# First dense pair in chunks of 512, 512 and 128 tokens, with a fourth accumulator and PSUM banks handed out by first free

## The chip, the cores and the metric

The kernel runs on one core of a Trainium2 chip. The metric is the device time of one execution in microseconds (us). The engines are PE (TensorE), DVE (VectorE), ACT (ScalarE), POOL (GpSimd) and SP (SyncE, which issues DMAs). PSUM, into which PE writes, has eight banks, each of which holds 512 float32 columns on 128 partitions.

## What is computed

An attention step makes 4608 tokens of 512 numbers; each token is routed to one of 8 experts, exactly 576 to each, in the order of the largest gate values that are left; the expert's two layers act on its tokens; then one dense network with a hidden width of 2048 acts on all of them.

```python
def _moe_ref(x, w_gate, w1, w2):        # x 4608 x 512, 8 experts, cap 576
    ...
    out[mask] = np.maximum(x[mask] @ w1[e], 0.0) @ w2[e]

def _moe2_ref(x, w_in, w_out):          # w_in 512 x 2048, w_out 2048 x 512
    h = x @ w_in
    relu6 = np.clip(h + 3.0, 0.0, 6.0)
    g = h * relu6 / 6.0
    return g @ w_out

def reference(q, k, v, phi, ...):
    x = attn_out.transpose(0, 2, 1, 3).reshape(B * S, H * D)
    return _moe2_ref(_moe_ref(x, ...), ...)
```

## The kernel before

The attention comes first and leaves the tokens in DRAM (`xd`) and the gate values in `LG`. Then the experts go in pairs P = 0 to 3: `l1(2P)`, `l2(2P)`, `l1(2P+1)`, `l2(2P+1)` are the two layers of the pair's experts, and `l34(P)` sends the pair's 1152 tokens (tile `yt`) through the dense network. Every product is made of three float16 matmuls (high times high, high times low, low times high), so a float32 operand is first split into a high and a low float16 part.

`l34(P)` cuts its 1152 tokens into three chunks of 384 (three groups of 128). For each chunk it goes through 16 pieces f of the hidden width. A step n = 16*chunk + f has a first part ("L3", 12 matmuls `p<-yt,wi` of 384 columns into one PSUM bank), then ACT (relu with scale), DVE (`h<-h,p`, min and product), ACT (high half) and POOL (low half) make the hidden tile `h`; `l4(n)` (9 matmuls `acc<-wo,h` of 512 columns) follows LAG = 2 steps later and adds into three accumulators, `acc0` to `acc2`, one bank each, one for each group of 128 tokens. After f = 15 ACT empties acc0 and acc2 and DVE acc1 into `y` tiles, and POOL writes them to the output by indirect DMAs (`out_dram<-y,ix`). The five banks left are one for the router (`rtp`) and four, tag "mm", for everything else (`p1`, `p2`, `p3`, transposes `xp`, maxima `amx`).

The dense weights are converted while the first pair runs: 16 pieces of w_in and 16 of w_out, float64 read as pairs of int32, go through four DVE instructions each (one TENSOR_SCALAR and three SCALAR_TENSOR_TENSOR `cva`), three of ACT and one of POOL (`wi`, `wo`). L3 of piece f waits for WI[f], `l4` for WO[f]. The scale of the pair's second expert is a chain too: DVE's maxima `ym`, then `sy_1m`, then a small matmul on PE (`amx<-ident,sy_1m`). The router of expert k (`route(k)`) runs through DVE and PE in small steps (`C`, `rtp`, ..., `OH`, `RH`) beside all this, and so do the loads and splits of the expert weights (`wst`, `wscr`, `w`).

Nobody writes the instruction order by hand: generators (`spawn`) are advanced by a clock model `CK` while the main loop issues matmuls, and each instruction goes to its engine's queue at that moment. So the order on each engine is fixed when the program is built, by the model's costs and by the conditions that a generator waits for. One of these conditions is a free "mm" bank: `mm_slot` keeps a queue `MMQ` of the four given out last and always takes the oldest.

Of the kernel before, what the change touches and what calls it, by code (L numbers as in the profile page):

```python
# [9 lines left out]
F32 = mybir.dt.float32  # L10
# [10 lines left out]
def attn_moe_kernel(ctx: ExitStack, tc: tile.TileContext, q, k, v, phi, w_gate, w1, w2, w_in, w_out, out):  # L21
# [68 lines left out]
    with tc.tile_pool(name="ald", bufs=2) as ald, tc.tile_pool(name="aw", bufs=2) as aw, \  # L90
# [322 lines left out]
        def x_mm(t, pool, tag, *gs):  # L413
            u, half = XO[t // 2], t % 2
            if gs != (1,):
                XP[t] = pool.tile([128, 2, 256], F32, name="xa", tag=tag, bufs={"qp": 2, "mm": 4}[tag])
            p = XP[t]
            for g in gs:
                for b, r in parts(u):
                    nc.tensor.matmul(p[r, g], AT[u][:, half, g, r], VB[b][:, g], start=True, stop=True)  # L420
# [190 lines left out]
    def need(cond):  # L611
        while not cond():
            due = min(max(t[0], t[3].t - t[1] if t[3] is not None else 0.0) for t in CK.tasks)
            CK.now = max(CK.now + 0.02, due)
            run()
# [10 lines left out]
    def fp16(n):  # L626
        return max(0.027, n / 2400.0 + 0.003)

    MMQ = []

    def mm_slot(done):
        while len(MMQ) >= 4:
            d = MMQ.pop(0)
            b, CK.busy = CK.busy, False
            need(lambda: d[0])
            CK.busy = b
        MMQ.append(done)

    def mm_tile(shape, name, done):
        mm_slot(done)  # L640
        return ps.tile(shape, F32, name=name, tag="mm", bufs=4)

    jpi = iT = rt.tile([128, 16], I32, name="iT")
    nc.gpsimd.iota(iT, pattern=[[1, 16]], base=0, channel_multiplier=0)
# [43 lines left out]
    def all_max(m, f):  # L688
        yield V_.t + HOP
        done = [False]  # L690
        while len(MMQ) >= 4 and not MMQ[0][0]:
            yield CK.now + 0.05
        p = mm_tile([128, 128], "amx", done)
        nc.tensor.matmul(p, m.bitcast(F32).to_broadcast([128, 128]), ident, start=True, stop=True)
        CK.now += 0.22
        yield CK.now + HOP
        V_.tensor_reduce(f, p, axis=AX.X, op=OP.max)
        done[0] = True
# [356 lines left out]
    def gathers():  # L1055
        for k in range(E):
            while k not in IDX or not XD[0]:
                yield CK.now + 0.5
            ix = IDX[k]
            xgs = []  # L1060

            rdy = []

            def fetch(i):
                n = 64 if i == 4 and k % 2 == 0 else 128
                if k == 0:
# [12 lines left out]
            if k == 0:
                G_.t = max(G_.t, XDT[0])  # L1080
            for i in range(depth):
                if k == 0 and i == 2:
                    while not SR[0]:
                        yield CK.now + 0.1
                fetch(i)
            XI.add(k)
            while k and L1D.get(k - 1, 0) < 8:
                yield CK.now + 0.3
            xt = wk.tile([128, 2, 4, CAP], F16, name="xt")
            nx = [0]  # L1090
            for i in range(5):
                while CK.now < rdy[i]:
                    yield rdy[i]
                _, n, xg = xgs[i]
                done = [False]
                while len(MMQ) >= 4 and not MMQ[0][0]:
                    yield CK.now + 0.05
                p = mm_tile([128, 4, 128], "xp", done)
                for c in range(4):
                    tr(p[:, c, :n], xg[:n, c * 128:(c + 1) * 128], ident[:n, :n])  # L1100
                o = slice(0, 128) if i < 4 else (slice(0, 64) if k % 2 == 0 else slice(64, 128))
                w = o.stop - o.start
                xs = slice(i * 128, i * 128 + w)

                def ev(p=p, o=o, xs=xs, done=done):
                    yield CK.now + HOP
                    A_.activation(xt[:, 0, :, xs], p[:, :, o], AF.Copy, scale=SX[0][:, 0:1])
                    GI[0] = True
# [12 lines left out]
            XT[k] = xt  # L1121
# [130 lines left out]
    def x_tiles(n):  # L1252
        for _ in range(n):
            if XN[0] == 2 * NT:
                break
            t, g = divmod(XN[0], 2)
            XN[0] += 1
            if g == 0:
                XC[:] = [[False]]
                mm_slot(XC[0])  # L1260
            x_mm(t, ps, "mm", g)
            CK.now += 0.435
            if g:
                x_ev(t)
                A_.t = max(A_.t, CK.now) + 0.5
                XC[0][0] = True
                XDT[0] = dma(0.73, A_.t)
            XD[0] = XN[0] == 2 * NT
# [123 lines left out]
    def l34(P):  # L1392
        inv = {}
        iv4 = rt.tile([128, 1], F32, name="iv4", bufs=2)
        pend = []
        acc = []

        def l4(n):
            ch, f = divmod(n, 16)
            g, ok = pend.pop(0)  # L1400
            need(lambda: f in WO)
            if f == 0:
                acc[:] = [ps.tile([128, 512], F32, name=f"acc{t}") for t in range(3)]
            need(lambda: ok[0] >= 1)
            for i, (wi, xi) in enumerate(((0, 0), (1, 0), (0, 1))):
                if xi == 1:
                    need(lambda: ok[0] >= 2)
                for t in range(3):
                    mm(acc[t], g[:, xi, t * 128:t * 128 + 128], WO[f][:, wi], f == 0 and i == 0, f == 15 and i == 2,
                       fp16(512))  # L1410
            if f == 15:
                a3 = list(acc)

                def ev():
                    yield CK.now + 0.1
                    os = []
                    for t in range(3):
                        T = 3 * ch + t
                        o = ybuf(T % 4)[:, 0:512]
                        s = inv[0][:, 2:3] if T < 4 else (iv4 if T == 4 else inv[1][:, 2:3])  # L1420
                        if t == 1:
                            V_.tensor_scalar(o, a3[t], s, None, op0=OP.mult)
                        else:
                            A_.activation(o, a3[t], AF.Copy, scale=s)
                        os.append(o)
                    yield max(A_.t, V_.t) - 0.3
                    for t, o in enumerate(os):
                        T = 3 * ch + t
                        yield CK.now + 0.6
                        if T < 4:  # L1430
                            ix = IDX[2 * P][:, T:T + 1]
# [10 lines left out]
                        scat.append(d)  # L1442
                spawn(ev(), first=True)

        for n in range(48):
            ch, f = divmod(n, 16)
            segs = (((0, 384, 0),), ((0, 192, 0), (192, 384, 1)), ((0, 384, 1),))[ch]
            if n == 0:
                need(lambda: 2 * P in YR)
                inv[0] = inv_of(2 * P)  # L1450
# [5 lines left out]
                V_.tensor_copy(iv4[64:128], inv[1][64:128, 2:3])  # L1456
            need(lambda: f in WI)
            done = [False]
            p = mm_tile([128, 384], "p3", done)
            i = 0  # L1460
            for c in range(4):
                for wi, xi in ((0, 0), (0, 1), (1, 0)):
                    mm(p, WI[f][:, wi, c], YT[P][:, xi, c, ch * 384:(ch + 1) * 384], i == 0, i == 11, fp16(384))
                    i += 1
            g = hbuf((0, 1, 2, 5)[n % 4]).bitcast(F16)[:, 0:768].rearrange("p (a n) -> p a n", a=2)
            ok = [0]
            pend.append((g, ok))

            def ev(n=n, p=p, g=g, ok=ok, done=done, segs=segs):
                yield CK.now + 0.1  # L1470
                r = hbuf((3, 4, 6, 7)[n % 4])[:, 0:384]
                for a, b, w in segs:
                    A_.activation(r[:, a:b], p[:, a:b], AF.Relu, bias=half_c, scale=inv[w][:, 1:2])
                yield A_.t + HOP
                V_.scalar_tensor_tensor(r, r, 1.0, p, op0=OP.min, op1=OP.mult)
                done[0] = True
# [6 lines left out]
            spawn(ev(), first=True)  # L1483
            if f == 15:
                YP[P] = ch + 1
            if n >= LAG:
                l4(n - LAG)
        return [lambda n=n: l4(n) for n in range(48 - LAG, 48)]

    for _ in range(3):  # L1490
        early()
# [42 lines left out]
```

## Time and profile before

| | |
|---|---|
| median of three runs | 1523.43 us (1518.27 to 1528.63) |
| the profiled execution: time, span | 1519.59 us, 1517.7 us |
| mean granted clock of PE | 0.975 of 2.4 GHz |
| busy in the span: PE, DVE, ACT, POOL | 92%, 55%, 48%, 32% |

The span runs from the first to the last instruction that the profiler saw; the execution's own time has 1.9 us around it. The page of the profile gives means over stages that have different limits, so the stretch in question is read by itself: the wait lists say who was waited for, the timelines show the instructions of one engine in order of time with the idle time before each in brackets, and the chain follows the end of the program back from releaser to releaser. Line L618 is the helper that records matmuls, L567 the one for DVE, ACT and POOL.

### The profile page before, as it was taken

The page shows a single profiled execution, that of the slowest core. Times are in us where ns is not written, and L with a number is a line of the kernel's source. Part 1 is how long each engine was busy: PE and PEld are TensorE (multiplying, and loading weights), DVE is VectorE, ACT ScalarE, POOL GpSimd, SP SyncE. Part 2 cuts the span into 40 slices and gives each one's busy share as a digit, 9 for nine tenths or more (in the row PEclk, how much of TensorE's full clock was granted, in tenths as well). Part 3 has the DMA queues.
Part 4 walks back from the last instruction along what each step waited for, and adds up shares of the span by engine and source line. Part 5 has one row for each costly group of instructions (what it writes and reads, how often), then busy time and mean ns, then how long its engine had stood idle before and what let it go on. Part 6 is the DMA issues. An engine that isn't in the chain of part 4 may idle for free.

```text
span 1517.7 us, 26287 instructions
## 1 busy us (share of the span) xinstructions
PE 1402.9 (92%) x10506; PEld 931.7 (61%) x10506; DVE 838.6 (55%) x1985; ACT 734.0 (48%) x1419; POOL 481.0 (32%) x557
## 2 busy tenths in 40 slices
PE   4778886898889999999999999999999999999997
PEld 3667765786444445897544458885545588855553
DVE  5788967899985973453158743522477335221111
ACT  3667655577763553453335533623346536233332
POOL 4555305134552533200224332102235311023232
PEclk9989996999999999999999999999999999999999
DMA  9865577355300420200003220200023102000000
GB/s 301 291 229 194 178 254 242 131 179 167 112 27 22 136 78 21 82 17 1 1 22 93 72 70 30 70 1 1 21 67 111 56 29 70 1 0 22 1 21 21
DMA packets 65913, 130.67 MB, mean 86 GB/s; under 512 B 5248, under 2 KB 35968, under 8 KB 65792
## 3 DMA queue, kind: packets, MB, share of 16 engines
q1 hardware_dynamic: 49808, 74.48, 14.9%
q0 software_dynamic: 15168, 52.96, 10.8%
q8 instruction: 82, 1.34, 0.4%
q10 hardware_dynamic: 816, 1.57, 0.3%
q14 instruction: 39, 0.32, 0.1%
HBM read 110.12 MB, written 18.87 MB: 85 GB/s over the span
## 4 chain that ended last, share of the span: by engine, by line
PE 64%; DVE 16%; issue 6%; ACT 6%; DMA 5%; POOL 3%; SPq 0%; ACTq 0%; POOLq 0%; DVEq 0%
PE p L618 37%; PE acc L618 19%; DVE cva L567 4%; PE xa L420 2%; DMA xg<-xd,ix 2%; DMA wst<-in_moe_w_dram,ei 2%; POOL h L567 1%; DVE h L567 1%; PE kvp L191 1%; PE rtp L794 1%; DMA kvt<-in_v_dram 1%; DVE OH L567 1%; ACT wscr L567 1%; ACT h L567 1%; DVE pm L138 1%
## 5 line engine op out<-in xcount | busy, mean ns | idle before, releaser
L618 PE MATMUL p<-yt,wi 128*128 128x384 f16 x2304 | 422.8, 327 | 0.0
L618 PE MATMUL acc<-wo,h 128*128 128x512 f16 x1728 | 418.0, 380 | 4.5 <-ACT h L567 4.0
L567 POOL TENSOR_TENSOR h<-h,h 128x384 f16<-128x384 f32 x192 | 183.7, 957 | 623.6 <-ACT h L567 449.6
L618 PEld LDWEIGHTS <-w 128*128 128x128 f16 x3072 | 339.6, 121 | 49.9 <-issue 4.3
L618 PEld LDWEIGHTS <-wi 128*128 128x128 f16 x2304 | 218.6, 98 | 155.7 <-issue 1.6
L567 DVE SCALAR_TENSOR_TENSOR h<-h,p 128x384 f32<-128x384 f32 x192 | 105.9, 551 | 332.6 <-ACT h L567 317.1
L567 ACT ACTIVATE h<-p,half_c,inv 128x384 f32<-128x384 f32 (+1 forms) x256 | 143.9, 587 | 301.2 <-PE p L618 293.3
L618 PEld LDWEIGHTS <-h 128*128 128x128 f16 x1728 | 163.7, 98 | 173.7 <-ACT h L567 5.6
L618 PE MATMUL p<-xt,w 128*128 128x288 f16 x1536 | 198.0, 288 | 3.7 <-DVE h L567 3.5
L618 PE MATMUL p<-h,w 128*128 128x288 f16 x1536 | 197.3, 288 | 4.3 <-DVE w L567 3.7
L567 ACT ACTIVATE h<-h 128x384 f16<-128x384 f32 x192 | 100.1, 521 | 117.8 <-DVE h L567 116.5
L567 POOL DMA_INDIRECT wst<-in_moe_w_dram,ei x64 | 66.2, 1035 | 110.2 <-DVE tot L567 33.8
L567 DVE SCALAR_TENSOR_TENSOR h<-p,h 128x288 f16<-128x288 f32 x128 | 57.3, 454 | 78.9 <-ACT h L567 78.9
L567 ACT ACTIVATE h<-p 128x288 f16<-128x288 f32 x128 | 52.1, 414 | 90.7 <-PE p L618 89.7
L567 DVE SCALAR_TENSOR_TENSOR w<-wst,s,w 128x512 f16<-128x512 f32 x124 | 94.5, 781 | 2.4 <-ACT w L567 2.4
L567 ACT ACTIVATE w<-wst,s 128x512 f16<-128x512 f32 x124 | 83.7, 715 | 8.5 <-DVE s L567 5.8
L567 DVE SCALAR_TENSOR_TENSOR cva<-dst,cva 128x512 int32<-128x512 int32 (+1 forms) x96 | 82.6, 881 | 0.4 <-ACT dst L567 0.2
L567 DVE TENSOR_REDUCE ym<-y 128x1 f32<-128x288 f32 x64 | 28.8, 450 | 93.8 <-ACT y L567 91.9
L567 ACT ACTIVATE wscr<-wst 128x1024 bf16<-128x1024 f32 x64 | 67.3, 1052 | 19.0 <-DMA wst<-in_moe_w_dram,ei 18.0
L567 ACT ACTIVATE y<-p 128x288 f32<-128x288 f32 x64 | 26.0, 406 | 96.3 <-PE p L618 92.8
L567 POOL DMA_INDIRECT xg<-xd,ix x35 | 36.4, 1040 | 75.1 <-PE xp L623 55.6
L191 PE MATMUL kvp<-kvt,A 128*64 128x128 f32 x576 | 44.6, 309 | 7.3 <-ACT A L170 3.0
(313 smaller groups left out, 1568.5 us busy)
## 6 DMA issues: line engine op xcount, KB each, us to landing
dst<-in_moe_w_out_dram SPq DMA_DIRECT2D x26, 512.0 KB, 3.6
qt<-in_q_dram SPq DMA_DIRECT2D x8, 1024.0 KB, 13.3
dq<-in_moe_w_in_dram SPq DMA_DIRECT2D x16, 512.0 KB, 4.9
xd<-xs SPq DMA_DIRECT2D x32, 256.0 KB, 5.1
kvt<-in_k_dram SPq DMA_DIRECT2D x7, 1152.0 KB, 5.4
kvt<-in_v_dram SPq DMA_DIRECT2D x7, 1152.0 KB, 12.4
dst<-in_moe_w_in_dram SPq DMA_DIRECT2D x15, 512.0 KB, 4.6
ph<-in_phi_dram SPq DMA_DIRECT2D x8, 576.0 KB, 11.0
```

What stands on the lines that cost most here:

```text
L138: nc.vector.tensor_reduce(pm, PH[b].rearrange("p h (r m) -> p h m r", m=M), axis=AX.X, op=OP.max)
L191: nc.tensor.matmul(p[i * 64:(i + 1) * 64, g, 0:128], A[:, hp, r, :], KV[b][:, :, hp, r * 64:(r + 1) * 64], start=(r == 0), stop=(r == R - 1))
L420: nc.tensor.matmul(p[r, g], AT[u][:, half, g, r], VB[b][:, g], start=True, stop=True)
L567: r = f(*a, **kw)
L618: nc.tensor.matmul(o, l, r, start=start, stop=stop)
L794: nc.tensor.matmul(p[:60, :32], C[:, 4 * t:4 * t + 4].rearrange("p t n -> p (t n)"), Bo[:, 4 * t:4 * t + 4].rearrange("p t e -> p (t e)"), ...
```

## The change

The first pair's three chunks have 512, 512 and 128 tokens (4, 4 and 1 groups); the other pairs keep 384. A chunk of four groups needs a fourth accumulator, which is one of the four "mm" banks, held until it has been emptied. Accumulators are emptied in reverse (the last group first), in all pairs, while the output DMAs stay in the order of the groups. In the last chunk of the first pair `l4` follows three steps behind. `mm_slot` takes whichever bank is free, the one longest unused first. The gather of expert 1 waits for the first splits of W1 of expert 1 before it takes their buffers.

```diff
+    MMS, MMU, MMN = [None] * 4, [0] * 4, [0]
+
+    def mm_free():
+        return [i for i in range(4) if MMS[i] is None or MMS[i][0]]
 
     def mm_slot(done):
-        while len(MMQ) >= 4:
-            d = MMQ.pop(0)
-            b, CK.busy = CK.busy, False
-            need(lambda: d[0])
-            CK.busy = b
-        MMQ.append(done)
+        b, CK.busy = CK.busy, False
+        need(mm_free)
+        CK.busy = b
+        i = min(mm_free(), key=lambda i: MMU[i])
+        MMN[0] += 1
+        MMS[i], MMU[i] = done, MMN[0]
+        return f"mm{i}"
...
-        while len(MMQ) >= 4 and not MMQ[0][0]:
+        while not mm_free():
...
+                while k == 1 and i > 1 and WC.get(2, (0,))[0] < i // 2:
+                    yield CK.now + 0.1
...
+        acc, held = [], []
+        CN = (4, 4, 1) if P == 0 else (3, 3, 3)
+        CT = (0, CN[0], CN[0] + CN[1])
...
             if f == 0:
-                acc[:] = [ps.tile([128, 512], F32, name=f"acc{t}") for t in range(3)]
+                acc[:] = [ps.tile([128, 512], F32, name=f"acc{t}") for t in range(min(3, CN[ch]))]
+                held[:] = [[False]]
+                if CN[ch] > 3:
+                    acc.append(mm_tile([128, 512], "acc3", held[0]))
...
-                    for t in range(3):
-                        T = 3 * ch + t
+                    for t in reversed(range(len(a3))):
+                        T = CT[ch] + t
...
                         if t == 1:
                             V_.tensor_scalar(o, a3[t], s, None, op0=OP.mult)
                         else:
                             A_.activation(o, a3[t], AF.Copy, scale=s)
-                        os.append(o)
+                        os.insert(0, o)
+                        if t == 3:
+                            yield A_.t
+                            hd[0] = True
...
-            if n >= LAG:
-                l4(n - LAG)
+            lag = LAG if n < 32 or P else 3
+            while nx[0] <= n - lag:
+                l4(nx[0])
+                nx[0] += 1
```

Since the order on every engine comes out of the model, the change moves instructions before the first dense pair too. Three places follow, each before and then after.

DVE while it ranks the tokens of expert 1 (`off` to `OH`, six `OH` tiles, each of which PE turns into six matmuls `rtp<-RH,OH`); `w` are the splits of W2 of expert 0, which `l2(0)` needs:

```order
L567 TENSOR_SCALAR hi<-sli 128x36
L567 TENSOR_TENSOR R_4274<-hi,iTf 128x180
L567 TENSOR_TENSOR RH<-R_4274,idt 128x360
L567 TENSOR_TENSOR OH<-lo,i_2717 128x768
L567 SCALAR_TENSOR_TENSOR cva<-dst,cva 128x512
L567 TENSOR_REDUCE ym<-y_4171 128x1
L567 TENSOR_TENSOR OH<-lo,i_2717 128x768
L567 SCALAR_TENSOR_TENSOR cva<-dst,cva 128x512
L567 TENSOR_TENSOR OH<-lo,i_2717 128x768
```

```order
L567 TENSOR_TENSOR RH<-R_4215,idt 128x360
L567 TENSOR_TENSOR OH<-lo,i_2717 128x768
L567 SCALAR_TENSOR_TENSOR w_2_4153<-wst_3675,s_0_3903,w_2_4153 128x512
L567 TENSOR_TENSOR OH<-lo,i_2717 128x768
L567 SCALAR_TENSOR_TENSOR w_2_4153<-wst_3675,s_0_3903,w_2_4153 128x512
L567 TENSOR_TENSOR OH<-lo,i_2717 128x768
L567 SCALAR_TENSOR_TENSOR w_3_4223<-wst_3699,s_0_3903,w_3_4223 128x512
L567 TENSOR_TENSOR OH<-lo,i_2717 128x768
L567 SCALAR_TENSOR_TENSOR w_3_4223<-wst_3699,s_0_3903,w_3_4223 128x512
```

The last four splits of W2 of expert 0 stood ahead of the ranking and now stand between its `OH` tiles; on PE, the first four groups of `rtp<-RH,OH` had 76 matmuls of `l2(0)` ahead of the fourth of them since the ranking began, and now the four stand in a block ahead of its first.

DVE ahead of `sy_1m`, the scale of expert 1, for which PE waits with `amx<-ident,sy_1m` after the first L3 matmuls:

```order
L567 TENSOR_REDUCE ym<-y_5258 128x1
L567 SCALAR_TENSOR_TENSOR cva<-dst,cva 128x512
L567 TENSOR_REDUCE ymx_5369<-ym 128x1
L567 TENSOR_SCALAR cva<-dst 128x512
L567 SCALAR_TENSOR_TENSOR cva<-dst,cva 128x512
L567 TENSOR_SCALAR sy_1m<-ymx_5369 128x1
```

```order
L567 TENSOR_REDUCE ym<-y_5293 128x1
L567 SCALAR_TENSOR_TENSOR cva<-dst,cva 128x512
L567 TENSOR_SCALAR cva<-dst 128x512
L567 TENSOR_REDUCE ymx_5406<-ym 128x1
L567 SCALAR_TENSOR_TENSOR cva<-dst,cva 128x512
L567 TENSOR_SCALAR sy_1m<-ymx_5406 128x1
```

Here little moved, but what stands ahead grew: from the routing of expert 0 (where both orders still agree) to `sy_1m`, DVE's queue held 56 SCALAR_TENSOR_TENSOR and 20 TENSOR_SCALAR of `cva`, and now holds 65 and 23; the other instructions ahead of it are the same ones. On PE, 27 matmuls of 384 columns stood between `l2(1)` and that `amx`; now 23 of 512.

ACT where the second chunk of the first pair ends and its accumulators are emptied (`y<-acc`):

```order
L567 ACTIVATE h_7104<-p_7057,half_c,inv_5964 128x384
L567 ACTIVATE w_0_7123<-wst_6792,s_2_7088 128x512 x2
L567 ACTIVATE y_7133<-acc_6125,inv_5338 128x512
L567 ACTIVATE y_7137<-acc_6127,inv_5964 128x512
L567 ACTIVATE h_7097<-h_7104 128x384
```

```order
L567 ACTIVATE wscr,wsq<-wst_7318 128x1024
L567 ACTIVATE y_7427<-acc_6194,inv_6008 128x512
L567 ACTIVATE h_7451<-p_7423,half_c,inv_6008 128x128
L567 ACTIVATE wscr,wsq<-wst_7367 128x1024
L567 ACTIVATE y_7466<-acc_6193,inv_6008 128x512
L567 ACTIVATE y_7470<-acc_6191,iv_5372 128x512
L567 ACTIVATE h_7487<-p_7464,half_c,inv_6008 128x128
```

The accumulator that the next chunk starts with was the first of two in a row; it is now the last of three, behind a `wscr` (the square of a freshly loaded piece of expert 3's weights, `wst`). On POOL, the four output DMAs of that chunk, two gathers `xg` and only two low halves `h<-h,h` now stand in one stretch, in which PE's steps have 128 tokens.

## Rows read from the trace of the kernel before

**Rows 1.** Stretches of the span: us, busy us of PE, PEld, DVE, ACT, POOL, clock, DMA.

```profile
256.00:294.00 38.00, 32.71 (x268) 27.06 (x268) 32.09 (x88) 19.14 (x39) 4.72 (x4) 0.93 0.41 132
294.00:325.00 31.00, 28.66 (x257) 22.37 (x257) 28.82 (x71) 18.35 (x34) 13.51 (x13) 1.00 0.50 162
325.00:358.00 33.00, 27.88 (x221) 26.02 (x220) 32.17 (x64) 28.24 (x61) 12.23 (x10) 0.98 0.51 166
358.00:381.00 23.00, 23.00 (x168) 17.49 (x167) 22.96 (x34) 15.66 (x29) 11.78 (x8) 0.88 0.64 202
381.00:393.00 12.00, 7.58 (x41) 4.29 (x40) 11.83 (x28) 7.37 (x14) 5.53 (x5) 0.90 0.42 133
393.00:456.00 63.00, 58.06 (x304) 28.98 (x301) 57.69 (x85) 44.94 (x79) 35.01 (x29) 0.99 0.18 57
```

**Rows 2.** PE waits from 223 to 456 us: total us, times, longest.

```profile
PE amx L694 <- DVE sy_1m L567: 4.4, 1, 4.4
PE acc L618 <- ACT h L567: 4.0, 4, 1.8
```

**Rows 3.** PE waits from 456 to 605 us.

```profile
PE rtp L951 <- DVE OH L567: 3.2, 2, 1.7
PE rtp L794 <- DVE C L567: 1.6, 2, 1.1
```

**Rows 4.** PE in order of time: start, us, instruction, idle before it.

```profile
294.04 0.28 PE L618 MATMUL p<-h,w 128*128 128x288 f16 x1 [0.62 <-ACT h L567]
...
301.83 0.29 PE L951 MATMUL rtp<-RH,OH 128*128 128x10 bf16 x6
301.98 1.88 PE L618 MATMUL p<-h,w 128*128 128x288 f16 x14
...
357.78 23.58 PE L618 MATMUL p<-h,w 128*128 128x288 f16 x169 [2.28 <-DVE w L567]
...
381.20 4.55 PE L618 MATMUL p<-yt,wi 128*128 128x384 f16 x27
...
390.17 0.46 PE L694 MATMUL amx<-ident,sy_1m 128*128 128x128 f32 x2 [4.42 <-DVE sy_1m L567]
390.46 2.90 PE L618 MATMUL p<-yt,wi 128*128 128x384 f16 x9
```

**Rows 5.** The chain that ended last: start, us, work.

```profile
577.16 1.95 PE p L618 x12
579.11 1.94 PE acc L618 x9
```

**Rows 6.** DVE in order of time, around sy_1m and the last conversion.

```profile
384.31 0.68 DVE L567 SCALAR_TENSOR_TENSOR cva<-dst,cva 128x512 int32<-128x512 int32 x1
384.91 0.41 DVE L567 TENSOR_SCALAR cva<-dst 128x512 int32<-128x512 int32 x1
...
387.86 1.31 DVE L567 TENSOR_SCALAR cva<-dst 128x512 int32<-128x512 int32 x1
...
389.69 0.14 DVE L567 TENSOR_SCALAR sy_1m<-ymx 128x1 int32<-128x1 int32 x1
...
444.66 1.66 DVE L567 SCALAR_TENSOR_TENSOR cva<-dst,cva 128x512 f32<-128x512 f32 x1
```

**Rows 7.** ACT in order of time, first dense pair.

```profile
462.02 1.25 ACT L567 ACTIVATE y<-acc,inv 128x512 f32<-128x512 f32 x2
...
568.00 1.06 ACT L567 ACTIVATE wscr<-wst 128x1024 bf16<-128x1024 f32 x1 [1.21 <-DMA wst<-in_moe_w_dram,ei]
```

**Rows 8.** POOL in order of time, first dense pair.

```profile
463.27 1.01 POOL L567 DMA_INDIRECT out_dram<-y,ix  x1 [0.16 <-ACT y L567]
...
561.07 0.98 POOL L567 DMA_INDIRECT wst<-in_moe_w_dram,ei  x1 [3.08 <-DVE ei L567]
...
575.55 0.96 POOL L567 DMA_INDIRECT xg<-xd,ix  x1 [1.63 <-DVE ix L567]
```

**Rows 9.** ACT at the end of the program.

```profile
1509.08 1.26 ACT L567 ACTIVATE y<-acc,inv 128x512 f32<-128x512 f32 x2 [3.52 <-PE acc L618]
```

More of the change, by code (lines that the diff above doesn't have):

```diff
@@ L415, in x_mm @@
             if gs != (1,):
-                XP[t] = pool.tile([128, 2, 256], F32, name="xa", tag=tag, bufs={"qp": 2, "mm": 4}[tag])
+                XP[t] = pool.tile([128, 2, 256], F32, name="xa", tag=tag, bufs=2 if tag == "qp" else 1)
             p = XP[t]
@@ L627, in fp16 @@
         return max(0.027, n / 2400.0 + 0.003)
-    MMQ = []
+    MMS, MMU, MMN = [None] * 4, [0] * 4, [0]
+    def mm_free():
+        return [i for i in range(4) if MMS[i] is None or MMS[i][0]]
     def mm_slot(done):
-        while len(MMQ) >= 4:
-            d = MMQ.pop(0)
-            b, CK.busy = CK.busy, False
-            need(lambda: d[0])
-            CK.busy = b
-        MMQ.append(done)
+        b, CK.busy = CK.busy, False
[5 more added lines that the diff above has]
+        return f"mm{i}"
     def mm_tile(shape, name, done):
-        mm_slot(done)
-        return ps.tile(shape, F32, name=name, tag="mm", bufs=4)
+        return ps.tile(shape, F32, name=name, tag=mm_slot(done))
     jpi = iT = rt.tile([128, 16], I32, name="iT")
@@ L1095, in gathers @@
                 done = [False]
-                while len(MMQ) >= 4 and not MMQ[0][0]:
+                while not mm_free():
                     yield CK.now + 0.05
@@ L1259, in x_tiles @@
                 XC[:] = [[False]]
-                mm_slot(XC[0])
-            x_mm(t, ps, "mm", g)
+                XC.append(mm_slot(XC[0]))
+            x_mm(t, ps, XC[1], g)
             CK.now += 0.435
@@ L1395, in l34 @@
         pend = []
-        acc = []
+        acc, held = [], []
+        CN = (4, 4, 1) if P == 0 else (3, 3, 3)
+        CT = (0, CN[0], CN[0] + CN[1])
         def l4(n):
@@ L1407, in l4 @@
                     need(lambda: ok[0] >= 2)
-                for t in range(3):
+                for t in range(CN[ch]):
                     mm(acc[t], g[:, xi, t * 128:t * 128 + 128], WO[f][:, wi], f == 0 and i == 0, f == 15 and i == 2,
@@ L1411, in l4 @@
             if f == 15:
-                a3 = list(acc)
+                a3, hd = list(acc), held[0]
                 def ev():
@@ L1416, in ev @@
                     os = []
-                    for t in range(3):
-                        T = 3 * ch + t
+                    for t in reversed(range(len(a3))):
+                        T = CT[ch] + t
                         o = ybuf(T % 4)[:, 0:512]
@@ L1424, in ev @@
                             A_.activation(o, a3[t], AF.Copy, scale=s)
-                        os.append(o)
+                        os.insert(0, o)
+                        if t == 3:
+                            yield A_.t
+                            hd[0] = True
                     yield max(A_.t, V_.t) - 0.3
                     for t, o in enumerate(os):
-                        T = 3 * ch + t
+                        T = CT[ch] + t
                         yield CK.now + 0.6
@@ L1443, in l4 @@
                 spawn(ev(), first=True)
+        nx = [0]
         for n in range(48):
             ch, f = divmod(n, 16)
-            segs = (((0, 384, 0),), ((0, 192, 0), (192, 384, 1)), ((0, 384, 1),))[ch]
+            w, c0 = 128 * CN[ch], 128 * CT[ch]
+            b = min(max(CAP - c0, 0), w)
+            segs = [x for x in ((0, b, 0), (b, w, 1)) if x[0] < x[1]]
             if n == 0:
@@ L1458, in l34 @@
             done = [False]
-            p = mm_tile([128, 384], "p3", done)
+            p = mm_tile([128, w], "p3", done)
             i = 0
@@ L1462, in l34, with ev @@
                 for wi, xi in ((0, 0), (0, 1), (1, 0)):
-                    mm(p, WI[f][:, wi, c], YT[P][:, xi, c, ch * 384:(ch + 1) * 384], i == 0, i == 11, fp16(384))
+                    mm(p, WI[f][:, wi, c], YT[P][:, xi, c, c0:c0 + w], i == 0, i == 11, fp16(w))
                     i += 1
-            g = hbuf((0, 1, 2, 5)[n % 4]).bitcast(F16)[:, 0:768].rearrange("p (a n) -> p a n", a=2)
+            g = hbuf((0, 1, 2, 5)[n % 4]).bitcast(F16)[:, 0:2 * w].rearrange("p (a n) -> p a n", a=2)
             ok = [0]
             pend.append((g, ok))
-            def ev(n=n, p=p, g=g, ok=ok, done=done, segs=segs):
+            def ev(n=n, p=p, g=g, ok=ok, done=done, segs=segs, w=w):
                 yield CK.now + 0.1
-                r = hbuf((3, 4, 6, 7)[n % 4])[:, 0:384]
-                for a, b, w in segs:
-                    A_.activation(r[:, a:b], p[:, a:b], AF.Relu, bias=half_c, scale=inv[w][:, 1:2])
+                r = hbuf((3, 4, 6, 7)[n % 4])[:, 0:w]
+                for a, b, e in segs:
+                    A_.activation(r[:, a:b], p[:, a:b], AF.Relu, bias=half_c, scale=inv[e][:, 1:2])
                 yield A_.t + HOP
@@ L1485, in l34 @@
                 YP[P] = ch + 1
-            if n >= LAG:
-                l4(n - LAG)
-        return [lambda n=n: l4(n) for n in range(48 - LAG, 48)]
+            lag = LAG if n < 32 or P else 3
+            while nx[0] <= n - lag:
+                l4(nx[0])
+                nx[0] += 1
+        return [lambda n=n: l4(n) for n in range(nx[0], 48)]
     for _ in range(3):
```

## The prediction, before the result was known

> **What bounds the kernel now.** I read the page first: PE is busy in nearly every slice after the first third, so the end is set by PE, and a change can gain only what PE loses to waiting. Next I cut out the stretches in which the first pair runs [rows 1]. PE is idle there for 5.3 us of 38, 2.3 of 31, 5.1 of 33, 0 of 23, 4.4 of 12 and 4.9 of 63: 22 us in all, 1.4% of the span. DVE has 5.9 and 2.2 us idle in the first two stretches, and then is full: 32.2 of 33, 23.0 of 23, 11.8 of 12, 57.7 of 63. From 325 us to the last conversion at 444.66 [rows 6] DVE sets the pace, with the conversion of the dense weights. Third, the list of waits says what this costs PE in the dense part: 4.4 us in one wait for sy_1m and 4.0 us in four waits of `acc` for a hidden tile that was late [rows 2]. After 456 us PE waits only for the router, 3.2 and 1.6 us [rows 3]. Without stalls the chain alternates L3 and `l4`, 1.95 and 1.94 us [rows 5], and that goes on to the end. So the question is when PE finishes the first pair.
>
> **The matmuls: 0.** L3 of a step is 12 matmuls of 384 in 1.95 us, 162.5 ns each, and `l4` is 9 of 512 in 1.94 us, 215.6 ns each [rows 5]. The line through both is 0.415 ns a column and 3 ns a matmul, which gives 56 ns for 128 columns. 2 x 215.6 + 56 = 487 ns stand against 3 x 162.5 = 487.5 ns, 192 times: no difference. `l4` has 432 matmuls as before. Each matmul loads weights of its own; six loads of 128 x 128 with six tiny matmuls pass in 0.15 us, 301.83 to 301.98 [rows 4], 25 ns each, so were none of a load hidden behind 128 columns, the third chunk would cost 192 x 25 = 4.8 us. Behind 288 and 384 columns loads are hidden; I take 0, the upper end is 4.8.
>
> In the Trainium skill, "TensorE: Matmul & The Clock Gate", section "Back-to-back issue gap", gives some 81 ns a matmul for a stream of loads and matmuls at 128 columns and 131 ns at 512. The second figure does not fit this trace (215.6 ns [rows 5]). By the first the third chunk would be longer by an estimated 192 x (81 - 56) = 4.8 us, and the sum 4.8 us higher.
>
> **Before the dense pair: 0 by itself.** The last four splits of W2 of expert 0 now stand between OH tiles, and PE has four groups of OH matmuls ahead of `l2(0)`, which began at 294.04 [rows 4]. It will begin some 8 us later: the 76 matmuls of 288 columns no longer ahead of the fourth group are 9.3 us at 0.122, by the same line [rows 5]. I book nothing, since DVE stays full and PE waits for DVE's pieces of W2 of expert 1 anyway, at 357.78 [rows 4]; if it isn't hidden, that is a rival below.
>
> **The wait for sy_1m: +4.3.** DVE has 9 SCALAR_TENSOR_TENSOR and 3 TENSOR_SCALAR more in its queue ahead of sy_1m. Spaced as at 384.31 to 384.91 they take 0.60 and some 0.33 us: 9 x 0.60 + 3 x 0.33 = 6.4. Three more pieces mean three more POOL subtractions beside DVE, and an instruction of 0.41 us takes 1.31 beside one [rows 6]: 0 to 2.7 us, I take 1.0. Against it, DVE idled 8.1 us in the first two stretches [rows 1], and work moved forward can fill that: 0 to 8.1, I take 2.5, because most of that idle time waits for router matmuls, which stay. So sy_1m comes 6.4 + 1.0 - 2.5 = 4.9 us later than 389.69, with ends of -1.7 and +9.1. PE does 23 x 0.2156 = 4.96 us ahead of it, where it did 27 x 0.1625 = 4.39: -0.6. What is queued behind the waiting matmul on PE is all of L3 and `l4`.
>
> **The waits in the first chunk: -3.0.** They are 4.0 us now. With 512 tokens a step of PE is 12 x 0.2156 x 2 = 5.2 us instead of 3.9, so a step leaves DVE a third more time, while there are as many conversions. They ought to vanish, but the late start leaves DVE's last h tiles among the conversions: I leave 1.0 us. Ends -4.0 and 0. Late next is the router, whose waits stay: 0, give or take 2.
>
> **The ends of the first two chunks: +4.9.** After the first chunk an L3 of 12 x 0.2156 = 2.6 us stands between the last `l4` and the next, and three ACT evictions at 0.63 [rows 7] are 1.9: they fit, 0.3 at a hop or a relu in between, 0 to 1. After the second chunk the L3 between is 12 x 0.056 = 0.7 us, and acc0, with which the third chunk starts, comes last of three evictions on ACT, behind a relu and a `wscr` of 1.06 us that waits for its DMA [rows 7]: 0.1 + 3 x 0.63 + 1.06 + 0.4 for the relu (128 columns, where the eviction has 512) = 3.5, less 0.7, 2.8; 0.5 if the evictions come early beside OH waits, 5 if the `wst` load that POOL issues late [rows 8] is late. Then POOL: four output DMAs and two gathers, 1.0 us each with gaps of 0.2 [rows 8], hold up the low halves for some 7 us; PE's step is 12 x 0.056 + 3 x 0.2156 = 1.3 us and it has three in hand: 7 - 1.3 - 3.9 = 1.8 us, 0 to 4.
>
> **The end of the program: +0.6.** The last three accumulators are emptied in reverse, and POOL's first output DMA wants the first group, now ACT's second eviction: half of 1.26 us [rows 9].
>
> **The router's waits: -0.5**, since some of them coincide with the new ones.
>
> Sum: 4.3 - 3.0 + 0.3 + 2.8 + 1.8 + 0.6 - 0.5 = +6.3 us on 1519.59, the profiled execution's own time: 1525.9, say 1526. That execution is 3.8 us below the median of the runs, which spread over 10 us. A change of 1% (15 us) is what a measurement of this kernel can tell from none; the forecast is no change.
>
> **Rivals.** (a) The gain: DVE fills all its idle time, sy_1m comes at 388, the first chunk never waits, and ACT and POOL are in time at the third: -1.7 - 0.6 - 4.0 + 0.5 + 0.6 - 2 = -7.2, so 1512. For it speaks that PE now has a third more work per piece of weights while DVE is the bound; against it, that those stalls are only 4.0 us and that sy_1m sits in the same DVE queue.
> (b) Slower, at `l2(0)`: the block of OH matmuls holds PE for 9.3 us, and after a long wait the granted clock is the lower level for a while (after the 4.42 us wait, 9 matmuls took 2.90 instead of 1.46 us [rows 4]; the stretch from 358, after 2.28 us of wait, has a mean of 0.88 [rows 1]): 9.3 + 3, less the 2.28 us wait that it hides, 10 us over the forecast, 1536. It decides if `l1(1)` then ends later than DVE's last split of W2 of expert 1.
> (c) Loads aren't hidden behind 128 columns: +4.8, 1531.
> (d) The fourth accumulator doesn't do its work: with three banks left for L3, PE waits for p where it waited for h. All of the 4.0 us stay, 1529. Against it: `l4(n)` two steps on needs the same DVE instruction that frees the bank.
>
> **How the numbers follow.** Forecast 0.50 (1520 to 1532), (a) 0.22, (b) 0.14, (c) 0.08, (d) 0.06. Above 1% slower (1535 on the profiled time) are half of (b) and an edge of the forecast and (c), 0.11; more than 1% faster would need two thirds of PE's 22 us, 0.04; the rest, 0.85, is within 1%. The range takes in (a) and most of (b), and leaves a tenth out on each side: 1511 to 1539.
>
> **What would show it.** In the changed profile: sy_1m's wait on PE of 5 us or more and its instruction after 393 us; no or one wait of `acc` for h before 450 us; `l2(0)` starting after 300; a wait of `acc` for an ACT eviction, and one for POOL, where the 128-column matmuls begin; those at 56 ns. The prediction is wrong if DVE's last conversion comes much before 440 us or after 455, or if the pairs after the first take another time than before.

## The result, and the profile of the changed kernel

The changed kernel takes 1538.59 us (median) against 1523.43 before: ratio 1.0108, 95% interval 1.0085 to 1.0131, some 16 us slower, where no change was forecast. One profiled execution of it was disturbed (1971.5 us); the rows below are of another one of the same kernel, 1537.13 us with a span of 1534.9.

The time up to the first scale matmul of expert 0 (`amx<-ident,s_0m`), in which all kernels here issue the same work, differs between executions by up to 9 us (last section), so places are compared from that matmul on. PE of the kernel before, in order of time: that matmul, the same for W2 of expert 0, the first L1 matmuls of expert 1 (the start of L3 is in [rows 4]).

```profile
244.72 0.77 PE L694 MATMUL amx<-ident,s_0m 128*128 128x128 f32 x2
...
275.62 0.49 PE L694 MATMUL amx<-ident,s_0m 128*128 128x128 f32 x2 [1.12 <-DVE h L567]
...
324.83 2.12 PE L618 MATMUL p<-xt,w 128*128 128x288 f16 x16
```

The same of the changed kernel, and further down the third chunk of the first pair:

```profile
246.12 0.77 PE L697 MATMUL amx<-ident,s_0m 128*128 128x128 f32 x2
...
284.97 0.49 PE L697 MATMUL amx<-ident,s_0m 128*128 128x128 f32 x2 [0.88 <-DVE h L567]
...
298.73 0.32 PE L954 MATMUL rtp<-RH,OH 128*128 128x10 bf16 x6 [4.61 <-DVE OH L567]
...
303.51 2.56 PE L618 MATMUL p<-h,w 128*128 128x288 f16 x10
...
335.97 4.82 PE L618 MATMUL p<-xt,w 128*128 128x288 f16 x38
...
359.93 0.78 PE L618 MATMUL p<-h,w 128*128 128x288 f16 x5
...
371.44 3.78 PE L618 MATMUL p<-h,w 128*128 128x288 f16 x15 [1.51 <-DVE w L567]
...
395.01 5.13 PE L618 MATMUL p<-yt,wi 128*128 128x512 f16 x23
403.67 0.46 PE L697 MATMUL amx<-ident,sy_1m 128*128 128x128 f32 x2 [3.53 <-DVE sy_1m L567]
...
599.25 1.44 PE L618 MATMUL acc<-wo,h 128*128 128x512 f16 x3 [2.80 <-ACT y L567]
...
600.68 1.44 PE L618 MATMUL p<-yt,wi 128*128 128x128 f16 x12
...
609.41 0.61 PE L618 MATMUL acc<-wo,h 128*128 128x512 f16 x1 [2.30 <-POOL h L567]
...
614.14 0.83 PE L618 MATMUL p<-yt,wi 128*128 128x128 f16 x12
...
615.46 0.83 PE L618 MATMUL p<-yt,wi 128*128 128x128 f16 x12
```

Counted from the first `amx` (l2(0) and l1(1) stand for the first matmul of that layer, L3 for the first matmul of the pair's dense part; span's end included; the kernels of the experiments stand here too, so that one table carries the places):

| kernel | l2(0) | l1(1) | L3, pair 0 | L3, pair 1 | L3, pair 3 | end |
|---|---|---|---|---|---|---|
| before | 49.3 | 80.1 | 136.5 | 461.8 | 1077.5 | 1273.0 |
| changed | 57.4 | 89.9 | 148.9 | 476.5 | 1092.6 | 1288.8 |
| banks only (e1) | 57.6 | 90.6 | 149.5 | 472.4 | 1088.8 | 1284.5 |
| before, strict scale (e10) | 57.3 | 89.9 | 149.0 | 470.5 | 1085.8 | 1281.5 |
| l2 in pieces (e6) | 49.2 | 88.2 | 146.3 | 477.7 | 1095.2 | 1291.5 |
| scale ahead (e7) | 48.4 | 81.0 | 135.3 | 469.3 | 1085.8 | 1282.0 |
| e7, forward, spaced (e9) | 50.3 | 83.1 | 136.4 | 465.6 | 1081.6 | 1277.3 |
| 512, 384, 256, sy first (e14) | 50.4 | 82.8 | 136.4 | 458.5 | 1074.3 | 1269.8 |

Of the 15.8 us, 12.4 are there when the dense part begins; 2.3 come in it; the pairs after it cost nothing (from L3 of pair 1 to L3 of pair 3, 615.7 us before and 616.1 now); the rest is the end of the program.

The windows of the changed kernel ([rows 1] before) show where: PE falls from 28.66 busy us to 21.66 between 294 and 325, and DVE, the supposed bound, from 28.82 to 23.93. The clock of 0.50 is the level of 1.2 GHz.

```profile
294.00:325.00 31.00, 21.66 (x180) 16.23 (x180) 23.93 (x54) 14.82 (x29) 11.88 (x9) 0.78 0.44 137
...
358.00:381.00 23.00, 16.59 (x96) 10.87 (x94) 22.90 (x30) 17.31 (x32) 12.39 (x9) 0.70 0.59 204
...
298.60:309.00 10.40, 6.65 (x58) 4.50 (x59) 9.06 (x16) 1.35 (x2) 5.15 (x4) 0.50 0.39 108
```

What PE waited for lies on DVE. Of DVE in order of time, first before (the scale of W2 of expert 0, its last split, and the last split of W2 of expert 1), then the changed kernel:

```profile
276.47 0.21 DVE L567 TENSOR_SCALAR s<-s_0f 128x1 int32<-128x1 int32 x2
...
289.57 0.73 DVE L567 SCALAR_TENSOR_TENSOR w<-wst,s,w 128x512 f16<-128x512 f32 x1
...
356.99 0.74 DVE L567 SCALAR_TENSOR_TENSOR w<-wst,s,w 128x512 f16<-128x512 f32 x1
```

```profile
285.82 0.21 DVE L567 TENSOR_SCALAR s<-s_0f 128x1 int32<-128x1 int32 x2
...
290.93 1.40 DVE L567 SCALAR_TENSOR_TENSOR w<-wst,s,w 128x512 f16<-128x512 f32 x2
297.72 0.95 DVE L567 TENSOR_TENSOR OH<-lo,i 128x768 bf16<-128x768 int32 x1
...
303.18 0.74 DVE L567 SCALAR_TENSOR_TENSOR w<-wst,s,w 128x512 f16<-128x512 f32 x1
...
369.75 1.64 DVE L567 SCALAR_TENSOR_TENSOR w<-wst,s,w 128x512 f16<-128x512 f32 x1
```

Counted from the first `amx`, the scale's own `amx` is 38.9 instead of 30.9, 8 us late; the last split ends at 57.8 instead of 45.6, 12.2 late, since four of the eight splits now stand behind the ranking of expert 1. The splits also free the staging buffers `wst` for the next load. POOL before, then POOL of the changed kernel, at the first loads of W1 of expert 1:

```profile
295.35 0.95 POOL L567 DMA_INDIRECT wst<-in_moe_w_dram,ei  x1 [7.71 <-DVE ei L567]
```

```profile
301.63 0.96 POOL L567 DMA_INDIRECT wst<-in_moe_w_dram,ei  x1 [19.78 <-DVE w L567]
304.20 3.24 POOL L567 DMA_INDIRECT wst<-in_moe_w_dram,ei  x1 [1.61 <-DVE w L567]
```

POOL waited for `ei` before; now it waits for the splits `w`, so expert 1's weights are loaded, squared, scaled and split later too. The last split of W2 of expert 1 ends at 125.3 instead of 113.0, 12.3 late, and PE goes on at once (357.78 in [rows 4], 371.44 now); from there to L3 it takes 23.4 us before and 23.6 now. So the 12.4 us reach the dense part through this split. Why DVE is less busy in 294 to 325 is shown only in part: of its idle time there the trace puts 1.2 us down to outputs `y` of l2(0) and 0.9 to the scale of W1 of expert 1, but also 2.0 to POOL's `wi` and 1.4 to the router.

### The profile page after: what moved, and what is told of

Same layout as the page of the kernel before. It is cut to its first block, busy times and chain, and to the rows that moved or that the text cites. A ratio compares the mean times of both kernels' runs of the same rounds, so it can differ in the third digit from the quotient of the medians.

```text
span 1969.3 us, 26287 instructions
## 1 busy us (share of the span) xinstructions
PE 1893.5 (96%) x10506; PEld 1097.4 (56%) x10506; DVE 844.7 (43%) x1984; ACT 742.4 (38%) x1420; POOL 481.7 (24%) x555
## 4 chain that ended last, share of the span: by engine, by line
PE 88%; issue 4%; DVE 4%; ACT 2%; DMA 1%; POOL 1%; POOLq 0%; ACTq 0%; SPq 0%; DVEq 0%
PE p L618 52%; PE acc L618 25%; PE xa L420 2%; PE kvp L191 2%; PE xp L623 1%; PE al L390 1%; DMA ph<-in_phi_dram 1%; PE rtp L797 1%; PE sc L341 1%; POOL h L567 1%; PE qp L317 1%; PE amx L697 0%; PE al L377 0%; PE rtp L806 0%; DVE pm L138 0%
## 5 line engine op out<-in xcount | busy, mean ns | idle before, releaser
L618 PE MATMUL acc<-wo,h 128*128 128x512 f16 x1728 | 571.3, 485 | 4.0 <-ACT y L567 2.8
L618 PE MATMUL p<-yt,wi 128*128 128x384 f16 (+2 forms) x2304 | 570.3, 408 | 0.0
L618 PEld LDWEIGHTS <-w 128*128 128x128 f16 x3072 | 410.1, 136 | 124.6 <-issue 2.5
L567 POOL TENSOR_TENSOR h<-h,h 128x384 f16<-128x384 f32 (+2 forms) x192 | 181.4, 946 | 914.1 <-ACT h L567 901.3
L618 PEld LDWEIGHTS <-wi 128*128 128x128 f16 x2304 | 250.8, 114 | 259.7 <-issue 111.4
L567 ACT ACTIVATE h<-p,half_c,inv 128x192 f32<-128x192 f32 (+5 forms) x256 | 144.4, 589 | 590.4 <-PE p L618 585.2
L567 DVE SCALAR_TENSOR_TENSOR h<-h,p 128x384 f32<-128x384 f32 (+2 forms) x192 | 106.2, 553 | 523.3 <-ACT h L567 521.1
L618 PE MATMUL p<-xt,w 128*128 128x288 f16 x1536 | 276.2, 357 | 0.2
L618 PE MATMUL p<-h,w 128*128 128x288 f16 x1536 | 272.0, 354 | 2.5 <-POOL w L567 1.3
L567 ACT ACTIVATE h<-h 128x384 f16<-128x384 f32 (+2 forms) x192 | 100.0, 521 | 105.5 <-DVE h L567 102.4
L567 DVE SCALAR_TENSOR_TENSOR h<-p,h 128x288 f16<-128x288 f32 x128 | 57.6, 456 | 143.1 <-ACT h L567 141.5
```

The source lines that it names most:

```text
L567: r = f(*a, **kw)
L618: nc.tensor.matmul(o, l, r, start=start, stop=stop)
```

## The experiments

**e0_after**: the changed kernel as it is.

> The changed kernel as it is, once more, for a profile that can be laid beside that of before. Theory (the prediction's steps with their sizes off): the extra 15 us arise between 294 and 460 us, as a late l2(0) (8 to 12 us, rival b of the prediction) and a wait for sy_1m of 5 us or more, and the pairs after the first take the time that they took before. Rival 1: the 15 us arise at the ends of the first two chunks (460 to 620 us), PE waiting for ACT's evictions and POOL's low halves: 8 us or more there. Rival 2: nothing arises in the first pair, and the later pairs, whose evictions are reversed, lose 4 to 5 us each.

The 12.4 us ahead of the dense part are there (l2(0) 8.1 late, l1(1) 9.8), the wait for sy_1m of 5 us isn't (3.53). Of rival 1 there are 2.80 and 2.30 us. Rival 2 falls.

**e1_banks_only**: `CN = (3, 3, 3)`, eviction forward, lag as before. The wait of expert 1's gathers stays.

> Only the handing out of banks by first free is kept: chunks of 384 in every pair, three accumulators, evictions in forward order. Theory (late l2(0), rival b): the block of OH matmuls ahead of l2(0) comes with the banks, so most of the loss is here already: 1530 to 1540 us. Rival 1 (the ends of the chunks of 512): this kernel is within 4 us of before, 1519 to 1528. Rival 2 (reversed evictions): the same, 1519 to 1528, with pairs 1 to 3 as before.

1534.21 us, ratio 1.0081 (1.0064 to 1.0098). The order of l2(0) and the loss come with the banks, without any chunk of 512.

**e7_scale_ahead**: the rule for booking is the suspect. Before, a tile that wanted a bank took the oldest entry out of the list before it waited for it, so the list was one short meanwhile, and an `amx` could be written out ahead. Now it has to find a bank that is free in the planner's model. The edit gives the old right back to `amx` alone:

```diff
+    MMW = [0]
     def mm_slot(done):
-        b, CK.busy = CK.busy, False
-        need(mm_free)
-        CK.busy = b
-        i = min(mm_free(), key=lambda i: MMU[i])
+        MMW[0] += not mm_free()
+        if MMW[0] < 2:
+            b, CK.busy = CK.busy, False
+            need(mm_free)
+            CK.busy = b
+            MMW[0] = 0
+        i = min(mm_free() or range(4), key=lambda i: MMU[i])
...
-        while not mm_free():
+        while not mm_free() and MMW[0] != 1:
             yield CK.now + 0.05
         p = mm_tile([128, 128], "amx", done)
```

> The changed kernel, save that the matmul which spreads a maximum over the partitions (amx) may be written out while a tile of L1 already waits for a bank, as it could before. Theory (late scale: the amx of W2 of expert 0 stands 46 matmuls later, so its splits come later on DVE and l2(0) later on PE): the order ahead of the dense pair is that of before again, l2(0) begins between 293 and 298 us, dense L3 within 3 us of 381, and what is left is what the chunks cost behind it (+3.4 us in the changed kernel's profile): 1521 to 1528. Rival 1 (the banks by first free cost time wherever they act, or the chunks do): 1532 or more. Rival 2 (only the block of OH matmuls on PE costs time, not the late scale): as the theory here; the next kernel tells these apart.

1532.77 us, ratio 1.0062 (1.0041 to 1.0083): 5 us over the theory's range, and at the edge of rival 1. PE of this kernel (its wait for sy_1m is named after ACT's `dst`, but DVE's second `sy_1m` instruction ends at 392.80, right before that matmul):

```profile
248.19 0.77 PE L702 MATMUL amx<-ident,s_0m 128*128 128x128 f32 x2
...
296.62 0.28 PE L618 MATMUL p<-h,w 128*128 128x288 f16 x1 [0.60 <-ACT h L567]
...
383.45 4.91 PE L618 MATMUL p<-yt,wi 128*128 128x512 f16 x22
392.95 0.76 PE L702 MATMUL amx<-ident,sy_1m 128*128 128x128 f32 x2 [4.59 <-ACT dst L567]
...
594.15 1.44 PE L618 MATMUL acc<-wo,h 128*128 128x512 f16 x3 [2.80 <-ACT y L567]
...
604.52 0.61 PE L618 MATMUL acc<-wo,h 128*128 128x512 f16 x1 [2.55 <-POOL h L567]
```

Both have a part. Ahead of the dense part the theory holds: L3 begins at 135.3, 1.2 us earlier than before. Behind it 10.2 us are lost (1146.7 to the end against 1136.5), where the changed kernel lost 3.4: the chunks with their reversed evictions cost 10 us by themselves. The two losses overlap, since `acc` waits less for `h` (1.2 us against 3.4 here) where the dense part begins 12 us late. At the end of the second chunk PE waits 2.80 and 2.55 us, and 1.91 ahead of them for an OH tile. Behind each of the three it runs in part or throughout at the lower clock, as windows of this kernel show (before, the clock is 1.00 from 450 to 605 us):

```profile
586.50:590.00 3.50, 3.49 (x21) 1.52 (x22) 3.50 (x5) 1.35 (x3) 1.52 (x2) 0.60 0.70 241
594.10:597.00 2.90, 2.85 (x22) 1.99 (x22) 0.00 (x0) 0.00 (x1) 1.01 (x1) 0.50 0.24 90
604.50:607.00 2.50, 2.48 (x16) 2.11 (x17) 0.51 (x3) 0.07 (x1) 2.19 (x4) 0.50 0.61 236
```

(12 matmuls of 128 columns take 1.44 there instead of 0.83.) At 0.60, 0.50 and 0.50 of the clock these stretches lose 3.5 x 0.40 + 2.9 x 0.50 + 2.5 x 0.50 = 4.1 us.

**e6_l2_in_pieces**: is it the block of 24 OH matmuls on PE, or the late scale? l2(0) no longer waits in the model for all of W2:

```diff
-            need(lambda: k in W2)
+            need(lambda: k in W2 or k == 0 and WC.get(1, (0,))[0] > 0)
...
+                    need(lambda: k in W2 or WC[1][0] > j // 2)
```

> The changed kernel, save that l2(0) is written out as soon as the first piece of W2 of expert 0 is split, not after the last one. The late scale stays, the block of 24 OH matmuls is broken up: 6 of l2(0)'s matmuls stand ahead of it and others between its groups. Theory (late scale): each tile of l2(0) needs all pieces of W2 within its first 24 matmuls, and the last split still stands behind OH tiles on DVE, so l2(0) begins early but its 76 matmuls in a row begin no earlier than 305 us: 1532 to 1539. Rival (the block itself): without it PE gains 8 us or more: 1523 to 1530.

1542.76 us, ratio 1.0115 (1.0077 to 1.0152): no better than the changed kernel. PE of this kernel:

```profile
250.13 0.77 PE L697 MATMUL amx<-ident,s_0m 128*128 128x128 f32 x2
...
299.29 0.90 PE L618 MATMUL p<-h,w 128*128 128x288 f16 x6 [1.12 <-DVE h L567]
...
313.55 9.47 PE L618 MATMUL p<-h,w 128*128 128x288 f16 x76
```

l2(0) begins at 49.2, as before the change, and still its 76 matmuls in a row begin at 63.4 (62.8 in the changed kernel). The block is a symptom.

**e10_before_strict_scale**: the other way round, the changed kernel's rule for the scale put into the kernel before.

```diff
-        while len(MMQ) >= 4 and not MMQ[0][0]:
+        while MMP or len(MMQ) >= 4 and not MMQ[0][0]:
             yield CK.now + 0.05
         p = mm_tile([128, 128], "amx", done)
```

(`MMP` holds the entry that a tile waits for.) Not shown is a second part of the edit, also from the changed kernel: the gathers of expert 1 wait for the pieces of weights whose buffers they take.

> The kernel before (banks in a queue, chunks of 384, three accumulators), with one rule taken from the change: the matmul which spreads a maximum (amx) isn't written out while a tile of L1 waits for a bank; and the two gathers into buffers of the weights' pieces wait for these pieces, as in the changed kernel. Theory (late scale): PE's order gets the block of 24 OH matmuls and the late amx, l2(0) begins 56 to 58 us after the first amx instead of 49.3, and the time is that of the kernel with the banks alone, 1531 to 1537. Rival (the loss lies in which bank a tile gets, and the late amx is a symptom): within 3 us of before, 1520 to 1527.

1531.83 us, ratio 1.0067 (1.005 to 1.0084), l2(0) at 57.3. With the queue of banks, chunks of 384 and three accumulators, this edit costs 10 us, so the rival falls. The gathers' wait isn't the cause by itself, since e7 keeps it and begins its dense part as early as before; the condition on the scale without that wait was not run.

**e8_ahead_forward**: e7 with `for t in range(len(a3))` and `os.append(o)`.

> The kernel with the scale ahead, and the accumulators emptied in forward order (acc0 first, the fourth last) in all pairs. Theory: PE's wait for ACT's y where the third chunk begins (2.80 us in the changed kernel) goes to 0.5 or less, the end of the program is 0.6 us earlier: 2 to 4 us below the kernel with the scale ahead. Rival (POOL is next): the low halves h are late anyway, PE waits for them instead, and the time is within 1 us of the kernel with the scale ahead.

1527.4 us, ratio 1.0035 (1.0018 to 1.0053), 5.4 us below e7 by the medians, 4.1 by the ratios. No wait for `y` is left; PE waits 3.1 us for POOL's `h` instead of 2.55, so the rival has a small part.

**e9_ahead_forward_spaced**: e8 with the output DMAs of that chunk apart.

```diff
-                        yield CK.now + 0.6
+                        yield CK.now + (2.0 if P == 0 and ch == 1 else 0.6)
```

> As the last one, and the output DMAs of the second chunk of the first pair are written out 2.0 us apart instead of 0.6, so that POOL's low halves of the third chunk stand between them. Theory: PE's wait for POOL's h in the third chunk (2.30 us in the changed kernel) goes too: 1 to 2.5 us below the last one, and 1516 to 1521 in all, below before. Rival: the gathers and output DMAs that now come later make L1 of the next expert or the router wait, and the time is as the last one or higher.

1525.8 us, ratio 1.0012 (0.9995 to 1.0029): the wait for POOL is 1.6 us, not gone, the theory's 1516 to 1521 is missed, and the kernel isn't below before.

**e11_chunks_432**: e9 with `CN = (4, 3, 2)`.

> The kernel with the scale ahead, forward order and spaced output DMAs, with chunks of 512, 384 and 256 tokens instead of 512, 512 and 128. Theory (a third chunk of 128 tokens gives POOL and ACT too little time a step, 1.32 us on PE): a step of 256 tokens takes 12 x 0.109 + 6 x 0.2156 = 2.6 us, the waits for ACT and POOL at the third chunk vanish and with them the matmuls at the lower clock behind them: 2 to 5 us below it, 1520 to 1524. Rival (what is left of the loss lies in the first chunk, at sy_1m and the waits of acc for h): within 1 us of it, 1525 to 1527.

1521.23 us, ratio 0.9992 (0.9974 to 1.001): 3 us below e9 by the ratios, but the two intervals overlap. No wait of `acc` is left between 460 and 625 us, and the clock there is 1.00. What the theory said of the waits holds.

**e12_before_sy_first** and **e13_spaced_sy_first**: the kernel before, and e9, with this ahead of each of DVE's four steps of a conversion (`aside()` is true from the sixth `ym` of expert 1 until sy_1m is written out):

```diff
+        while aside():
+            yield CK.now + 0.1, V_
```

> The kernel before, with the conversions of dense weights on DVE standing aside from the sixth ym of expert 1 to sy_1m: three or four SCALAR_TENSOR_TENSOR and one or two TENSOR_SCALAR of cva that stood ahead of sy_1m now stand behind it. Theory (the wait for sy_1m is DVE's queue, as in the prediction): sy_1m comes 2 to 3 us earlier, PE's wait of 4.4 us becomes 1.5 to 2.5, and half of that or more stays to the end: 1519 to 1522. Rival (given back): the conversions come later by as much, the waits of acc for h in the first chunk grow from 4.0 to 6 us or more, and the time is that of before within 1 us.

1522.24 us, ratio 1.0001 (0.9988 to 1.0014). The list of PE's waits, 376 to 456 us (before: [rows 2]):

```profile
PE acc L618 <- POOL h L567: 3.9, 2, 3.3
PE rtp L794 <- DVE C L567: 2.9, 1, 2.9
PE acc L618 <- ACT h L567: 2.2, 4, 0.8
PE amx L694 <- DVE sy_1m L567: 0.8, 1, 0.8
PE acc L618 <- POOL wo L567: 0.6, 1, 0.6
```

The 4.4 us for sy_1m are 0.8, and all of it is given back as waits for `h` and `C`: the rival.

> The kernel with the scale ahead, forward order and spaced output DMAs, and the conversions standing aside in the same way. Theory: the wait for sy_1m (6.2 us there) becomes 3 to 4 us, and the first chunk of 512 tokens, with 5.2 us a step, hides the later conversions: 2 to 3 us below it, 1522 to 1524, no better than before. Rival (given back): acc waits for h as much longer, 1525 to 1527.

1519.77 us, ratio 0.9992 (0.9973 to 1.0011), 3 us below e9 by the ratios, with intervals that overlap again: with a first chunk of 512 the earlier sy_1m seems to stay. PE no longer waits for it in the trace; the theory had left 3 to 4 us.

**e14_432_sy_first** and **e15_384_sy_first**: e13 with `CN = (4, 3, 2)`, and with chunks of 384 throughout (lag as before).

> The kernel with chunks of 512, 384 and 256 tokens (scale ahead, forward order, spaced output DMAs), and the conversions standing aside for sy_1m. Theory (the two terms lie at different places and add up): 1516 to 1519, below before by 2 to 5 us. Rival (given back: the later conversions make acc wait for h, as in the kernel before with the same step): 1520 to 1523, no better than before.

1518.03 us, ratio 0.9975 (0.9957 to 0.9993): 4 us below before, the only kernel here that beats it.

> The same with chunks of 384 in all pairs and three accumulators, so that of the change only the banks by first free are left, with the scale ahead. Theory (512 tokens in the first chunk give DVE a third more time a step, so that the conversions which stood aside are hidden): 2 to 4 us slower than the kernel with chunks of 512, 384 and 256, 1520 to 1523. Rival (the size of the first chunk changes nothing): within 1 us of it.

1521.62 us, ratio 0.9998 (0.998 to 1.0015), 3.5 us above e14. PE's waits from 376 to 456 us, e14, then e15:

```profile
PE acc L618 <- ACT h L567: 4.2, 4, 2.0
PE acc L618 <- POOL h L567: 2.2, 1, 2.2
PE amx L702 <- DVE sy_1m L567: 1.7, 1, 1.7
```

```profile
PE acc L618 <- ACT h L567: 8.0, 6, 2.3
PE amx L702 <- DVE sy_1m L567: 1.3, 1, 1.3
PE acc L618 <- POOL h L567: 0.4, 1, 0.4
```

`acc` waits 6.4 us for `h` where it waits 8.4 with chunks of 384: 2.0 of the 3.5 us lie in the first chunk. Behind it e15 waits 2.7 us for C, which e14 doesn't, so not all of the difference is shown to come from the size of the first chunk, and the two intervals overlap.

## Why the prediction was wrong

**The step that failed is "Before the dense pair: 0 by itself".** It measured 12.4 us at the start of the dense part. By the end of the program it is worth 6.8 us (15.8 in the changed kernel, 9.0 in e7, which undoes it), most of the 9.5 us by which the sum of 6.3 fell short. Its reason was that "DVE stays full and PE waits for DVE's pieces of W2 of expert 1 anyway". DVE didn't stay full (23.93 of 31 us), and those pieces are 12.3 us late themselves, since the loads of expert 1's weights wait for the splits of W2 of expert 0, whose scale is 8 us late. I took DVE for a bound of its own where it was one link of a loop from PE's `amx` over DVE's splits, POOL's loads and back to PE. The order had shown that `amx` 46 matmuls of L1 later; the prediction looked at the OH matmuls behind it. Undone alone (e7), the 12.4 us are -1.2; put into the kernel before (e10), they are 12.5, of which 8.5 are left at the end of the program.

**Rival (b) had nearly the size (10 us over the forecast), not the cause.** Its block of OH matmuls can be broken up and nothing is gained (e6). Its condition, l1(1) ending later than DVE's last split of W2 of expert 1, wasn't met either: l2(1) began at 113.8 and still waited for these splits. That its 1536 lies close to the 1537.13 of the profiled execution is luck, and so is it that the stated range, widened for (b), just holds the result. A chance of 0.14 was too small for a shift that the order showed in full.

**The matmuls: right.** A step of the third chunk takes 615.46 - 614.14 = 1.32 us; less 3 x 0.2156, 12 matmuls take 0.673 us, 56 ns each. Rival (c) falls. The Trainium skill, "TensorE: Matmul & The Clock Gate", section "Wait — 56ns, not 53.3ns?", gives 55.6 ns at 128 columns for the higher clock, and the trace agrees; the 81 ns of the section "Back-to-back issue gap", which the prediction weighed, don't hold here.

**The wait for sy_1m: +4.3 was too much.** It is 0.9 us shorter in the changed kernel, whose dense part begins late; with the start as before it is 4.0 to 6.5 us (4.02, 4.59, 6.2 and 6.5 in e8, e7, e9 and e11), so -0.4 to +2.1. No run here tells which of the three terms of that sum is off.

**The waits in the first chunk: -3.0, right in the changed kernel**: 4.0 us of waits of `acc` for ACT's `h` [rows 2] became none, and 1.2 us for POOL's, where 0.3 had been. With the start as before they are 3.4 in all (e7), so the reason given, a third more time a step, holds for 0.9 of it, and the late start for the rest. **The router's waits: -0.5**; OH 3.2 became 3.5 and C 1.6 became 0.4 [rows 3].

**The ends of the chunks: the waits right, a term missing.** 2.80 us for ACT's `y` was forecast as 2.8, POOL's 2.30 as 1.8, the first end as 0.3 (no wait seen). ACT of the changed kernel stands as the order said, a `wscr` between the evictions and the one that PE needs last:

```profile
595.67 0.69 ACT L567 ACTIVATE y<-acc,inv 128x512 f32<-128x512 f32 x1
...
596.90 1.04 ACT L567 ACTIVATE wscr<-wst 128x1024 bf16<-128x1024 f32 x1
...
597.94 0.68 ACT L567 ACTIVATE y<-acc,inv 128x512 f32<-128x512 f32 x1
598.51 0.68 ACT L567 ACTIVATE y<-acc,iv 128x512 f32<-128x512 f32 x1
```

Missing is the clock behind such waits, 4.1 us in e7. I had priced it in rival (b) and not here. The chunks cost 10.2 us in e7, where the sum had 6.3; it came that near because its +4.3 for sy_1m, 0.2 in e7, made up for the clock. The Trainium skill, "TensorE: Matmul & The Clock Gate", section "HAM oscillation — how this bites in real kernels", tells of a kernel that pays a stretch at half clock after every wait. The trace agrees for the three waits of e7; in the changed kernel the same wait of 1.91 us for OH was followed by a clock of 1.00 (last section).

**The end of the program: +0.6, right.** The first output DMA starts 1.54 us after ACT's first of the last evictions (1527.50 against 1525.96), before 0.96. **Rival (d) falls**: no wait of `p` for a bank shows in the dense part. **Rival (a)** has at most a part in e14: with a larger first chunk, and a third that isn't so small that ACT and POOL can't follow, it is 3.5 us below e15, 2.0 of them seen as shorter waits in the first chunk.

## What to carry to other kernels

Where a scheduler writes the order, compare first the place of the smallest instructions, scales and flags, on which whole queues hang: here one tiny matmul 46 matmuls later cost 10 us. An engine that is full is a bound only if what it does next doesn't wait for the engine that waits for it; follow that loop once round before booking 0. A tail chunk should be so large that its step on the fastest engine covers the fixed costs of the slower ones, and a wait should be priced with the lower clock that can stand behind it.

## What the runs showed of the hardware

Waits of PE of only 1.9 to 2.8 us were followed by the level of 1.2 GHz in e7 (0.60, 0.50 and 0.50 in the windows above), and so cost another 1.2 to 1.5 us each. Not every such wait was: in the changed kernel PE waits 1.91 us for OH up to 593.21, and stays at the level of 2.4 GHz:

```profile
592.70:596.00 3.30, 2.79 (x34) 1.73 (x35) 3.30 (x5) 1.94 (x6) 2.02 (x2) 1.00 0.75 206
```

And the executions differ by up to 9 us before the first scale matmul, which begins between 241.70 (e12) and 250.56 us (e15) although the same work stands ahead of it (2260 matmuls in each kernel). That may be most of the 10 us spread of the runs; with one profile of each kernel it isn't shown. Places further on are better compared from that matmul than from the span's start.
